# Attention with beacons, then a maxout FFN: three requests and two casts move one cluster up, and a batch's FFN units are dealt out in another order

## The chip, the cores and the metric

The kernel runs on one core of one Trainium2 chip. The metric is the device time of one execution in microseconds (us); lower is better. The kernel before takes 288.83 us, the median of three runs (288.78 to 288.86).

A core has TensorE (PE: matmuls, and the loads of their weights, PEld), VectorE (DVE), ScalarE (ACT) and GpSimd (POOL), each of which works through its own instructions in order, and SyncE (SP), which only asks for transfers. POOL asks for transfers too, for those that change the number type on the way. PSUM, where matmuls write, has eight banks of 512 fp32 columns; a bank can be written again when what stood in it has been read out by ACT or DVE.

## What is computed

```python
# attention: 8 batches, 8 heads, 576 tokens, 64 wide; 16 beacon keys and values ahead of the others
k_all = concat([beacon_k, k]);  v_all = concat([beacon_v, v])
scores = q @ k_all.T / sqrt(64), causal on the 576 keys
a = exp(scores - max);  a /= a.sum()
x = (a @ v_all) laid out as 4608 tokens x 512
# FFN: 512 -> 768 -> 512
h = maximum(maximum(x @ w1, x @ w2), x @ w3)
out = h @ w_out
```

## The kernel before

**Attention.** Two heads make a pair; there are 32 pairs, four to a batch, and two pairs make a quad. For a pair, q and k come in with tokens on partitions and have to be turned (head width on partitions) into the tiles `qT` and `kT`. `turn_pair` (L456) does it by 24 small matmuls with the identity into two PSUM banks; `evac_k` (DVE) and `evac_q` (DVE or ACT) copy them out. `place_beacons` (L445) puts 16 beacon columns ahead of `kT`. `emit_burst` (L522) computes all the scores of a pair in four groups, each in two neighbouring banks, and issues five exponentials on ACT. `emit_masks` (L540) zeroes on POOL what causality forbids. `emit_pv_whole` (L614) multiplies the weights of a quad with V into four banks, ACT copies the raw results and inverts the sums, and the returned `finish` multiplies the two on DVE into `xT`, the FFN's input.

Batch 0 goes by halves: `emit_pv` with `invert_sums` (ACT), which queues products, and `multiply` (DVE), which does them, out of banks 4 and 5. `finish_pv` is both in a row.

**FFN.** A unit is one PSUM result of the FFN: `mm1_unit` (L720), four matmuls of 512 tokens for one of six row blocks of `hT` and one of the three weights; `mm1_halves` (L731), the same work as two row blocks of 256 tokens, used for the first 512 tokens, half of which are there earlier; `mm2_unit` (L750), six matmuls with `w_out_sb`, whose result goes to the output. The first weight's result is cast into `hT`, the second's and third's are joined by `tensor_max` on DVE. With `end`, a unit is split over two banks that are evacuated one by one; in the main loop the last unit of each stretch is given that way, in the pair of banks that `last_pair` (L155) names. Each 512 tokens have 22 units; `units` (L794) lists them in the order in which they are given out, and `emit_ffn` gives out the next one. For the first 512 tokens: 0 to 5 are halves of the first 256 tokens, 6 to 11 of the others, 12 to 17 the third weight, 18 to 21 the second product, which needs `w_out_sb`.

**Order.** All of it is written out by hand: an engine does its instructions in the order in which the code issues them.

- `first_batch` (L903) does batch 0, with units between (`F`), turns pair 4, and asks for batch 1's V (`load_v`; the first of the two pieces stands behind a memset of DVE, its gate).
- `second_batch` (L988) runs a cluster for each of the pairs 4 to 7: beacons of the next pair, burst, masks, turning of the next pair, units (3, 3, 2, 2). Then follow the PV of quad 2, the turning of pair 8 and two units.
- The main loop (L1035) takes the pairs from 8 on: burst, a PV at every even pair, masks, then units; after the first unit the next pair is turned, after the second POOL casts and asks for later pairs. Pair 8 has two units, 18 and 19, with the turning of pair 9 between them.

**Transfers.** `load_cast(p)` (L252) asks on POOL for q and k of a pair, cast to bf16 on the way, into a place in `quad` tiles that the pair four before has left. Pairs 4 to 7 are asked for in `first_batch`. Pair 8 is asked for ahead of pair 7's masks, `w_out` (`load_w_out`, L344) and pair 9 behind the second of them. Batch 1's V lands in fp32 and POOL casts it into `v_sb` in two pieces (`cast_v`, L308): the first, row blocks 0 to 2, behind pair 6's masks, the second, blocks 3 and 4, behind pair 7's second mask. `next_load` then asks on SP for pairs 10 and 11, batch 2's V and pair 12; the first of these stands behind a memset of POOL, its gate.

Of the kernel before, what the change touches and what calls it, by code (L numbers as in the profile page):

```python
# [17 lines left out]
def kernel(  # L18
# [13 lines left out]
    nc = tc.nc  # L32
# [8 lines left out]
    n_ft = d_ff // 128  # L41
# [19 lines left out]
    PPB = H // 2  # L61
# [142 lines left out]
    by_act = nc.scalar.copy  # L204
# [482 lines left out]
    def finish_pv():  # L687
        invert_sums()
        multiply()
# [38 lines left out]
            else:  # L728
                (by_act if hi < TOKB else by_dve)(h[:, lo:hi], ps[:, lo:hi])  # L729

    def mm1_halves(tb, ft, i, lo, hi, new_ps):  # L731
        if tb not in hTs:
            hTs[tb] = ffn_h.tile([128, n_ft, TOKB], BF16, name="hT")
        h = hTs[tb][:, ft : ft + 2, lo:hi]
        ps = new_ps().rearrange("p (f c) -> p f c", f=2)
        for f in range(2):
            for ct in range(n_ct):
                nc.tensor.matmul(  # L738
                    ps[:, f],
                    w_in[i][:, ct, 128 * (ft + f) : 128 * (ft + f + 1)],  # L740
                    xT[:, ct, tb * TOKB + lo : tb * TOKB + hi],
                    start=(ct == 0),
                    stop=(ct == n_ct - 1),
                )
        if i == 0:
            by_dve(h, ps)
        else:
            nc.vector.tensor_max(h, h, ps)

    def mm2_unit(tb, tt, new_ps, end=False):  # L750
        hT = hTs[tb]
# [43 lines left out]
    for tb in range(n_tokb):  # L795
        need = 2 * ((TOKB * (tb + 1) - 1) // S) + 1
        if tb == 0:
            for n, lo in ((0, 0), (need, MID)):
                for i in range(2):
                    for ft in range(0, n_ft, 2):  # L800
                        units.append((n, mm1_halves, (tb, ft, i, lo, lo + MID)))
        for ft in range(n_ft):
            for i in range(2 if tb == 0 else 0, 3):
                units.append((need, mm1_unit, (tb, ft, i)))
        for tt in range(TOKB // 128):
            units.append((need, mm2_unit, (tb, tt)))
    END = len(units)
# [88 lines left out]

    S_, T, M, P, V = emit_scores, turn_part, emit_masks, emit_pv, cast_first_v

    def F(n=1, new_ps=ffn_psum.tile):
        for _ in range(n):  # L900
            assert emit_ffn(END, new_ps)

    def first_batch():  # L903
        S_(0, 0)
# [70 lines left out]
        M(3, 3, True)  # L975
        F()
        turn_beacons(1, B_PE, bk16_1)
        P(1, 1)
        finish_pv()
        F()  # L980
        turn_pair(PPB, by_act)
        load_v(1, 0, nc.vector)
        load_v(1, 1)
        place_beacons(PPB, by_act)
        F(2)
        free_banks[:] = [2, 3, 0, 1, 4, 5, 6, 7]

    def second_batch():  # L988
        for p in range(PPB, 2 * PPB):
            last = p == 2 * PPB - 1  # L990
            place_beacons(p + 1, by_act)
            emit_burst(p)
            if last:
                load_cast(2 * PPB)
            for gi in range(NG):
                emit_masks(p, gi)
                if last and gi == 1:
                    cast_v(1, 1, by_pool)
                    load_w_out()
                    load_cast(2 * PPB + 1)  # L1000
                    next_load(gate=nc.gpsimd)
                    next_load(4)
            if p == 2 * PPB - 2:
                cast_v(1, 0, by_pool)
            if not last:
                turn_pair(p + 1, by_dve)
            F(3 if p < PPB + 2 else 2, next_psum)
        finish = emit_pv_whole(n_quad)
        turn_pair(2 * PPB, by_dve)
        F(2, next_psum)  # L1010
        finish()
# [93 lines left out]
```

## Time and profile before

| | us |
|---|---|
| median of 3 runs | 288.83 |
| profiled execution, whole time | 290.4 |
| its span, first to last instruction | 288.7 |
| TensorE busy | 277.3 (96%) |
| DVE busy | 172.3 (60%) |
| ACT busy | 159.6 (55%) |
| POOL busy | 136.7 (47%) |

The mean granted TensorE clock is 0.994 of full speed. In the span, batch 0's end lies at about 25 to 31 us, the clusters of pairs 4 to 7 at 31 to 47, the PV of quad 2 at 47 to 50, pair 8 from 53 on and pair 9 from 64 on.

The profile is of one execution. A row of the timeline gives start, length, engine, line of the code, operation, output and inputs, sizes, and in brackets how long the engine had been idle and what ended that; neighbouring instructions of one line are merged in a row, with their count. A row of the waits gives who waited for whom, the total, how many times, and the longest. A row of the windows gives for a stretch the busy time and count of each engine, the granted clock, the mean busy share of the 16 DMA engines and the GB/s. A row of the DMA issues gives the size and the time from request to landing.

### The profile page before, as it was taken

To read this page: it belongs to the slowest core of one execution; us is meant where nothing else is said; L and a number is where in the kernel's file an instruction comes from. 1 tells how busy PE (TensorE), PEld (TensorE's weight loads), DVE (VectorE), ACT (ScalarE), POOL (GpSimd) and SP (SyncE) were. 2 spreads that over 40 slices of the span, in tenths; PEclk is the share of its full clock that TensorE was granted. 3 is DMA by queue.
4 is the path that set the end of the run, shared out by engine and by line. 5 is a ranking of instruction groups with operands and counts; after the bars stand their busy time and mean duration, and the time that the engine had idled before them with its cause. 6 is when DMAs were issued, how large, how long until landed. Compare 5 with 4: busy or idle time off the path is not lost.

```text
span 288.7 us, 7758 instructions
## 1 busy us (share of the span) xinstructions
PE 277.3 (96%) x3068; PEld 157.3 (54%) x3068; DVE 172.3 (60%) x303; ACT 159.6 (55%) x299; POOL 136.7 (47%) x282
## 2 busy tenths in 40 slices
PE   7889998879999999999999999999999999999995
PEld 3457764445555565555555787555555554444442
DVE  3774864537484748464836383638464847885873
ACT  3597586845859576666666666756675640000000
POOL 7298249628558592648465845584336210000000
PEclk9999999979999999999999999999999999999999
DMA  8999952999999799999999999899752003003004
GB/s 156 200 184 192 215 118 41 185 239 255 291 247 209 217 232 242 178 234 248 262 213 201 259 231 250 182 198 232 179 144 91 0 2 115 32 1 145 0 2 145
DMA packets 85316, 48.84 MB, mean 169 GB/s; under 512 B 64416, under 2 KB 80032, under 8 KB 85280
## 3 DMA queue, kind: packets, MB, share of 16 engines
q1 hardware_dynamic: 78176, 42.22, 64.5%
q0 software_dynamic: 6544, 5.80, 13.2%
q8 instruction: 24, 0.39, 0.6%
q10 hardware_dynamic: 560, 0.33, 0.5%
q14 instruction: 12, 0.10, 0.1%
HBM read 35.13 MB, written 14.22 MB: 171 GB/s over the span
## 4 chain that ended last, share of the span: by engine, by line
PE 85%; DMA 6%; POOL 2%; DVE 2%; issue 2%; ACT 1%; POOLq 0%; DVEq 0%; ACTq 0%
PE acc L709 44%; PE acc L757 16%; PE acc L633 9%; PE acc L513 7%; DMA quad<-in_k_dram 6%; PE acc L738 4%; PE acc L404 2%; PE acc L600 1%; DVE at_sb L551 1%; PE acc L498 1%; POOL quad L256 1%; POOL at_sb L553 1%; POOL v_sb L320 1%; ACT at_sb L531 0%; DVE kT L433 0%
## 5 line engine op out<-in xcount | busy, mean ns | idle before, releaser
L709 PE MATMUL acc<-xT,w_sb 128*128 128x512 bf16 (+4 forms) x744 | 135.5, 338 | 0.0
L553 POOL TENSOR_SCALAR_AFFINE_SELECT at_sb<-at_sb 128x256 bf16<-128x256 bf16 (+2 forms) x176 | 64.4, 386 | 85.8 <-ACT at_sb L531 79.6
L727 DVE TENSOR_TENSOR hT<-hT,acc 128x512 bf16<-128x512 bf16 x102 | 70.0, 687 | 58.4 <-PE acc L709 53.5
L709 PEld LDWEIGHTS <-w_sb 128*128 128x128 bf16 x744 | 69.1, 98 | 59.5
L531 ACT ACTIVATE at_sb<-acc 128x208 bf16<-128x208 f32 (+3 forms) x140 | 89.5, 737 | 8.2 <-PE acc L513 7.0
L757 PE MATMUL acc<-w_out_sb,hT 128*128 128x512 bf16 (+2 forms) x246 | 49.7, 355 | 0.8 <-DMA w_out_sb<-in_moe_w_out_dram 0.8
L764 DVE COPY y<-acc 128x512 f32<-128x512 f32 (+1 forms) x35 | 22.0, 629 | 23.9 <-PE acc L757 12.9
L275 POOL CAST p<-st 96x768 bf16<-96x768 f32 x44 | 35.0, 822 | 1.9 <-DMA st<-in_q_dram 1.0
L757 PEld LDWEIGHTS <-hT 128*128 128x128 bf16 x246 | 23.2, 100 | 23.2 <-DVE hT L727 1.6
L729 ACT CAST hT<-acc 128x352 bf16<-128x352 f32 x18 | 8.1, 452 | 47.3 <-PE acc L709 47.3
L729 DVE CAST hT<-acc 128x512 bf16<-128x512 f32 (+1 forms) x48 | 26.6, 554 | 9.7 <-PE acc L709 9.5
L513 PE MATMUL acc<-qT,kT 64*128 64x208 bf16 (+1 forms) x336 | 27.0, 282 | 0.9 <-DVE hT L727 0.4
L782 ACT COPY y<-acc 128x320 f32<-128x320 f32 x1 | 0.4, 426 | 46.0 <-PE acc L775 46.0
L633 PE MATMUL acc<-at_sb,v_sb 128*32 128x512 bf16 (+5 forms) x672 | 23.2, 281 | 0.6 <-POOL v_sb L320 0.6
L513 PEld LDWEIGHTS <-kT 64*128 64x128 bf16 x336 | 15.4, 94 | 13.6 <-issue 3.8
L656 DVE TENSOR_TENSOR xT<-raw,recip 128x576 bf16<-128x576 f32 x28 | 20.9, 788 | 0.0
L633 PEld LDWEIGHTS <-v_sb 128*32 128x32 bf16 (+1 forms) x672 | 14.5, 96 | 7.8 <-POOL v_sb L320 1.2
L320 POOL CAST v_sb<-st 128x1536 bf16<-128x1536 f32 (+2 forms) x21 | 18.2, 894 | 0.0
L643 ACT COPY raw<-acc 128x512 f32<-128x512 f32 x28 | 15.8, 637 | 3.7 <-PE acc L633 3.5
L507 ACT ACTIVATE at_sb<-acc 128x1024 bf16<-128x1024 f32 (+3 forms) x16 | 13.1, 859 | 3.9 <-PE acc L498 3.8
L633 PE MATMUL acc<-at_sb,ones 128*32 128x512 bf16 (+3 forms) x336 | 14.9, 284 | 0.0
L451 DVE COPY kT<-acc 128x576 bf16<-128x576 bf16 x12 | 9.0, 753 | 8.5 <-PE acc L404 8.5
(73 smaller groups left out, 178.7 us busy)
## 6 DMA issues: line engine op xcount, KB each, us to landing
out_dram<-y SPq DMA_DIRECT2D x35, 256.0 KB, 3.4
st<-in_q_dram SPq DMA_DIRECT2D x22, 288.0 KB, 4.5
st<-in_k_dram SPq DMA_DIRECT2D x22, 288.0 KB, 4.8
st<-in_v_dram SPq DMA_DIRECT2D x24, 256.0 KB, 6.4
w_sb<-in_moe_w_dram POOLq DMA_DIRECT2D x6, 384.0 KB, 6.7
q_dram<-p SPq DMA_DIRECT2D x16, 144.0 KB, 2.4
k_dram<-p SPq DMA_DIRECT2D x16, 144.0 KB, 2.2
st<-in_v_dram SPq DMA_DIRECT2D x8, 224.0 KB, 6.6
```

The lines of the kernel that those rows point to most:

```text
L275: cast(t16.rearrange("p r h d -> p h r d"), st[0:QP, i * NQ2 : (i + 1) * NQ2].rearrange("p (h r d) -> p h r d", h=2, r=QR),)
L320: cast(v_sb[0:n, t:t1].rearrange("p t h d -> p (t h d)"), st[0:n, (t - t_lo) * H * D : (t1 - t_lo) * H * D],)
L513: nc.tensor.matmul(ps, kTs[p % NT][hs, 128 * t : 128 * t + 128], qTs[p % NT][hs, q0:q1], start=True, stop=True, tile_position=(64 * e, 0),)
L531: nc.scalar.activation(out=both_heads(p, gi)[:, e0:e1], in_=acc[:, first + e0 : first + e1, 0 : g_width(p, gi)], func=AF.Exp, scale=scale,)
L553: nc.gpsimd.affine_select(out=view, in_=view, compare_op=ALU.is_ge, fill=0.0, base=x0, pattern=[[0, 2], [1, hi - lo]], channel_multiplier=-1,)
L633: nc.tensor.matmul(acc[32 * j : 32 * j + 32, bank, lo + q0 - qa : lo + qb - qa], lhsT, at_view(PPQ * quad + j // 2, t, j % 2, q0, qb), sta ...
L656: nc.vector.tensor_mul(xT[:, 2 * g + i, c0 : c0 + S], raw[:, i], recip)
L709: nc.tensor.matmul(ps[:, a:b], w_in[i][:, ct, 128 * ft : 128 * (ft + 1)], xT[:, ct, x0 : x0 + b - a], start=(ct == 0), stop=(ct == n_ct - 1),)
L727: nc.vector.tensor_max(h[:, lo:hi], h[:, lo:hi], ps[:, lo:hi])
L729: (by_act if hi < TOKB else by_dve)(h[:, lo:hi], ps[:, lo:hi])
L757: nc.tensor.matmul(ps[:, lo:hi], hT[:, ft, 128 * tt : 128 * (tt + 1)], w_out_sb[:, ft, lo:hi], start=(ft == 0), stop=(ft == n_ft - 1),)
L764: (by_act if hi < d_model else by_dve)(y[:, lo:hi], ps[:, lo:hi])
```

## The change

Pair 8 is asked for ahead of pair 5's masks, `w_out` and pair 9 ahead of pair 6's. V's first piece is cast behind pair 6's second mask, the second behind pair 6's last, and the gate with the loads behind it follows there. Of the first 512 tokens' units `first_batch` gives out five instead of six, and the clusters 3, 3, 3 and 2; in the first three clusters the last unit goes to two banks. For that `mm1_halves` gets the form `end`: one bank for each of its two row blocks, each evacuated by itself, the first weight's by ACT. The order of the units puts a half unit at each of these places. At the end of batch 0, beacons of pair 4 are placed ahead of the last PV, and the products of that PV are issued behind the turning of pair 4 and the loads of V, no longer ahead of a unit and the turning.

```diff
-    def mm1_halves(tb, ft, i, lo, hi, new_ps):
+    def mm1_halves(tb, ft, i, lo, hi, new_ps, end=False):
...
-        h = hTs[tb][:, ft : ft + 2, lo:hi]
-        ps = new_ps().rearrange("p (f c) -> p f c", f=2)
+        whole = None if end else new_ps().rearrange("p (f c) -> p f c", f=2)
         for f in range(2):
+            ps = new_ps()[:, 0 : hi - lo] if end else whole[:, f]
...
-        if i == 0:
-            by_dve(h, ps)
-        else:
-            nc.vector.tensor_max(h, h, ps)
+            if not end and f == 0:
+                continue
+            h = hTs[tb][:, ft + f, lo:hi] if end else hTs[tb][:, ft : ft + 2, lo:hi]
+            ps = ps if end else whole
+            if i > 0:
+                nc.vector.tensor_max(h, h, ps)
+            else:
+                (by_act if end else by_dve)(h, ps)
...
-            for n, lo in ((0, 0), (need, MID)):
-                for i in range(2):
-                    for ft in range(0, n_ft, 2):
-                        units.append((n, mm1_halves, (tb, ft, i, lo, lo + MID)))
-        for ft in range(n_ft):
-            for i in range(2 if tb == 0 else 0, 3):
-                units.append((need, mm1_unit, (tb, ft, i)))
+            order = [(0, f, 0) for f in (0, 2, 4)] + [(0, f, 1) for f in (0, 2, 4)]
+            order += [(MID, 0, 0), (MID, 2, 0), (MID, 0, 1), (MID, 2, 1), (MID, 4, 0)]
+            for lo, ft, i in order:
+                units.append((need if lo else 0, mm1_halves, (tb, ft, i, lo, lo + MID)))
+            for ft in range(n_ft):
+                units.append((need, mm1_unit, (tb, ft, 2)))
+            units.insert(len(order) + 2, (need, mm1_halves, (tb, 4, 1, MID, 2 * MID)))
+        else:
+            for ft in range(n_ft):
+                for i in range(3):
+                    units.append((need, mm1_unit, (tb, ft, i)))
...
-    def F(n=1, new_ps=ffn_psum.tile):
+    def F(n=1, new_ps=ffn_psum.tile, close=False):
         for _ in range(n):
-            assert emit_ffn(END, new_ps)
+            assert emit_ffn(END, new_ps, close)
...
         turn_beacons(1, B_PE, bk16_1)
+        place_beacons(PPB, by_act)
         P(1, 1)
-        finish_pv()
+        invert_sums()
         F()
         turn_pair(PPB, by_act)
         load_v(1, 0, nc.vector)
         load_v(1, 1)
-        place_beacons(PPB, by_act)
-        F(2)
+        multiply()
+        F()
...
         for p in range(PPB, 2 * PPB):
-            last = p == 2 * PPB - 1
             place_beacons(p + 1, by_act)
             emit_burst(p)
-            if last:
+            if p == PPB + 1:
                 load_cast(2 * PPB)
+            if p == PPB + 2:
+                load_w_out()
+                load_cast(2 * PPB + 1)
             for gi in range(NG):
                 emit_masks(p, gi)
-                if last and gi == 1:
-                    cast_v(1, 1, by_pool)
-                    load_w_out()
-                    load_cast(2 * PPB + 1)
-                    next_load(gate=nc.gpsimd)
-                    next_load(4)
-            if p == 2 * PPB - 2:
-                cast_v(1, 0, by_pool)
-            if not last:
+                if p == PPB + 2 and gi == 1:
+                    cast_v(1, 0, by_pool)
+            if p == PPB + 2:
+                cast_v(1, 1, by_pool)
+                next_load(gate=nc.gpsimd)
+                next_load(4)
+            if p + 1 < 2 * PPB:
                 turn_pair(p + 1, by_dve)
-            F(3 if p < PPB + 2 else 2, next_psum)
+                F(2, next_psum)
+                F(1, last_pair(), True)
+        F(2, next_psum)
         finish = emit_pv_whole(n_quad)
```

More of the change, by code (lines that the diff above doesn't have):

```diff
@@ L729, in mm1_unit @@
                 (by_act if hi < TOKB else by_dve)(h[:, lo:hi], ps[:, lo:hi])
-    def mm1_halves(tb, ft, i, lo, hi, new_ps):
+    def mm1_halves(tb, ft, i, lo, hi, new_ps, end=False):
         if tb not in hTs:
             hTs[tb] = ffn_h.tile([128, n_ft, TOKB], BF16, name="hT")
-        h = hTs[tb][:, ft : ft + 2, lo:hi]
-        ps = new_ps().rearrange("p (f c) -> p f c", f=2)
+        whole = None if end else new_ps().rearrange("p (f c) -> p f c", f=2)
         for f in range(2):
+            ps = new_ps()[:, 0 : hi - lo] if end else whole[:, f]
             for ct in range(n_ct):
                 nc.tensor.matmul(
-                    ps[:, f],
+                    ps,
                     w_in[i][:, ct, 128 * (ft + f) : 128 * (ft + f + 1)],
```

## The prediction

> **What bounds the kernel now.** I read the page first, then TensorE's waits, then the stretch in which they lie, in windows and instruction by instruction. "Cluster" is the work of one pair of heads in the loops of batches 1 and 2: burst of scores, five exponentials (ACT), masks (POOL), turning of the next pair, FFN units.
>
> ```profile
> span 288.7 us, 7758 instructions
> PE 277.3 (96%) x3068; PEld 157.3 (54%) x3068; DVE 172.3 (60%) x303; ACT 159.6 (55%) x299; POOL 136.7 (47%) x282
> ```
>
> TensorE is busy 96% of the span. Its waits between 40 and 72 us:
>
> ```profile
> PE acc L404 <- DMA quad<-in_k_dram: 1.2, 1, 1.2
> PE acc L757 <- DMA w_out_sb<-in_moe_w_out_dram: 0.8, 1, 0.8
> PE acc L633 <- POOL v_sb L320: 0.6, 2, 0.3
> ```
>
> The same view from 62 us to the end names no wait of TensorE at all. So what is won before 62 us is kept, as long as loads and casts come sooner by as much; what is won on another engine alone is worth nothing. The stretch in windows (PE, PEld, DVE, ACT, POOL busy, granted clock, DMA share, GB/s):
>
> ```profile
> 44.00:46.00 2.00, 1.80 (x16) 0.92 (x17) 0.88 (x2) 1.72 (x4) 2.00 (x4) 1.00 0.00 0
> ...
> 62.00:64.00 2.00, 2.00 (x14) 1.30 (x14) 0.11 (x2) 0.45 (x1) 0.00 (x0) 0.50 1.33 213
> ```
>
> The DMA engines stand still before the late requests are made, and after the waits the granted clock is 0.50. TensorE in order of time (start, length); L513 is a burst, L633 a PV, L404 a turning, L709 and L757 the FFN's two products:
>
> ```profile
> 43.92 0.81 PE L513 MATMUL acc<-qT,kT 64*128 64x208 bf16 x7
> ...
> 45.23 1.90 PE L709 MATMUL acc<-xT,w_sb 128*128 128x512 bf16 x8
> 47.07 0.86 PE L633 MATMUL acc<-at_sb,ones 128*32 128x512 bf16 x20
> ...
> 50.30 0.70 PE L404 MATMUL acc<-ident,quad 96*64 96x96 bf16 x24
> 50.94 1.90 PE L709 MATMUL acc<-xT,w_sb 128*128 128x512 bf16 x8
> 52.77 0.81 PE L513 MATMUL acc<-qT,kT 64*128 64x208 bf16 x7
> ...
> 54.08 0.87 PE L633 MATMUL acc<-at_sb,ones 128*32 128x512 bf16 x20
> ...
> 63.74 1.27 PE L513 MATMUL acc<-qT,kT 64*128 64x208 bf16 x12
> 64.94 1.47 PE L757 MATMUL acc<-w_out_sb,hT 128*128 128x512 bf16 x6
> 66.24 0.68 PE L404 MATMUL acc<-ident,p 96*128 96x96 bf16 x12
> ```
>
> And the same work where nothing disturbs it:
>
> ```profile
> 71.61 0.92 PE L513 MATMUL acc<-qT,kT 64*128 64x208 bf16 x12
> 72.46 0.86 PE L633 MATMUL acc<-at_sb,ones 128*32 128x512 bf16 x20
> ...
> 74.71 1.04 PE L709 MATMUL acc<-xT,w_sb 128*128 128x512 bf16 x4
> ```
>
> I count from start to start, since a matmul's tail hides the beginning of a wait: a burst takes 72.46 - 71.61 = 0.85, a PV 74.71 - 72.46 = 2.25, a unit of the second product 66.24 - 64.94 = 1.30, a turning from `quad` 50.94 - 50.30 = 0.64.
>
> **The requests made sooner.** Three terms.
>
> First, PV of quad 2 runs 50.30 - 47.07 = 3.23, 0.98 over 2.25: the two waits for batch 1's values. Now POOL casts them behind pair 7's first mask and ahead of its requests:
>
> ```profile
> 44.73 1.46 POOL L320 CAST v_sb<-st 128x1536 bf16<-128x1536 f32 x1
> ...
> 48.16 1.16 POOL L320 CAST v_sb<-st 128x512 bf16<-128x512 f32 x2
> 49.27 0.85 POOL L345 DMA_DIRECT2D w_out_sb<-in_moe_w_out_dram  x1
> ```
>
> After the change the first cast stands between pair 6's masks and the second right behind them. POOL then has, from the end of pair 5's masks, w_out's request (0.85), pair 9's two, two masks, 1.46, two masks, 1.16. Starting at about 40, with some 1.3 for pair 9's requests and 0.9 for two masks, the second cast ends at about 46.5, before TensorE is at the fourth row block of V (some 1.2 us into the PV). **-0.98**. Queued behind these on POOL are pair 7's masks and the memset that gates SP's loads of pairs 10 to 12 and batch 2's V: they come at about 47, now behind pair 9's requests and so after 51. Pair 6's masks are late by about 1 us, with no reader before 53. Pair 8's requests go ahead of pair 5's masks, in time that POOL spends waiting for exponentials; without that cover they would put the masks back by 1.3, which still nothing reads before 47.
>
> Second, from the start of quad 3's PV to pair 9's burst now takes 63.74 - 54.08 = 9.66: w_out is waited for, then pair 9's q and k, and the closing unit runs at half clock. Undisturbed it is 2.25 + 1.30 + 0.64 + 1.30 = 5.49. What the requests took to land:
>
> ```profile
> w_out_sb<-in_moe_w_out_dram POOLq DMA_DIRECT2D x1, 768.0 KB, 7.9
> ...
> quad<-in_k_dram POOLq DMA_DIRECT2D x1, 144.0 KB, 9.9
> ```
>
> Requested at 40 to 42 and landing at these times they are there by 52, and are needed at about 56 and 57. **-4.17**. Next in line is ACT, which must finish quad 2 and 3's sums before it can copy pair 9's qT:
>
> ```profile
> 58.11 0.68 ACT L651 ACTIVATE recip<-recip 128x576 f32<-128x576 f32 x1
> ...
> 63.04 0.45 ACT L764 COPY y<-acc 128x352 f32<-128x352 f32 x1 [2.74 <-PE acc L757]
> ```
>
> That chain began with pair 8's burst at 52.77 and ends 58.11 + 0.68 - 52.77 = 6.02 after it; a copy of 576 columns (0.75 on DVE, in a row below) brings it to 6.77, against 54.08 - 52.77 + 5.49 = 6.80 on TensorE. So TensorE just doesn't wait; the closing unit's 0.45 on ACT comes behind that copy and delays no one. If it did wait, I'd expect 0.2.
>
> Third, pair 9's burst at half clock took 64.94 - 63.74 = 1.20 for 0.85: **-0.35**, as the idle stretch ahead of it is gone.
>
> Pair 8's requests move into the time in which batch 1's V is being fetched:
>
> ```profile
> L304 SPq DMA_DIRECT2D st<-in_v_dram x5: 431/907/3907, 31.0 to 37.0; - x5
> ```
>
> ```profile
> st<-in_v_dram SPq DMA_DIRECT2D x1, 160.0 KB, 4.3
> ```
>
> ```profile
> quad<-in_k_dram POOLq DMA_DIRECT2D x1, 144.0 KB, 3.3
> ```
>
> The last piece of V, asked for at 37.0, lands at 41.3, and its cast is due at about 45.3; so I price this at nothing, with 4 us of cover. The two requests of pair 8 landed in 3.3 us each, over some 4 us together, with the engines to themselves. The Trainium skill ("DMA: Bandwidth & Descriptors", section "Issuing engines are not separate DMA queues") says that requests of different queues end up on the same 16 engines and interleave: by it V would land up to those 4 us later, at 45.3, and the sum would still be the same, with the cover used up; no run here yet shows the two together.
>
> **The end of batch 0 and the new order of units.** Units are only dealt out differently (five instead of six ahead of pair 4, then 3, 3, 3, 2), and a half unit of two products is as long as a whole unit, so TensorE's work is the same; what changes is who waits.
>
> ```profile
> 29.26 1.92 PE L738 MATMUL acc<-xT,w_sb 128*128 128x256 bf16 x16
> 31.11 1.21 PE L513 MATMUL acc<-qT,kT 64*128 64x208 bf16 x12
> ...
> 32.93 2.78 PE L738 MATMUL acc<-xT,w_sb 128*128 128x256 bf16 x24
> 35.65 0.68 PE L513 MATMUL acc<-qT,kT 64*128 64x208 bf16 x6
> ```
>
> ```profile
> 28.46 0.89 DVE L679 TENSOR_TENSOR xT<-acc,recip 128x288 bf16<-128x288 f32 x3 [1.63 <-ACT recip L669]
> ...
> 29.86 0.75 DVE L451 COPY kT<-acc 128x576 bf16<-128x576 bf16 x1
> ...
> 31.22 0.69 DVE L748 TENSOR_TENSOR hT<-hT,acc 128x512 bf16<-128x512 bf16 x1
> ```
>
> Today DVE does the products (0.89), a unit, kT, two units, done at 31.91, and the burst's last group starts behind that. After the change DVE begins with the unit, at about 28.8 (it ends on TensorE a turning, 0.64, before 29.26): 0.6 later comes kT, out at 30.15, so pair 4's burst starts at 30.2; then the three products, to about 30.96, and their banks hold the burst's third group; then the fifth unit's maximum, to 31.56, and its bank holds the fourth group, 0.3 long. The burst is over at about 31.9, and after the turning (0.64) units start at 32.55, against 32.93 now, with one unit of 0.9 fewer behind them. The reordering gives back most of what it seems to bring. The beacons' copy for pair 4 goes to where ACT waits for the PV; uncovered it would cost 0.15 (the row of two, below).
>
> In the clusters after that, exponentials set the pace:
>
> ```profile
> 29.65 0.31 ACT L447 COPY kT<-bT 128x16 bf16<-128x16 bf16 x2
> 31.47 3.19 ACT L531 ACTIVATE at_sb<-acc 128x208 bf16<-128x208 f32 x5 [1.51 <-PE acc L513]
> ```
>
> Units start 32.93 - 31.47 = 1.46 after the first exponential, which comes 0.36 after its burst, because they take the banks of its second group; then 35.65 - 32.93 = 2.72 to the next burst: 4.54 in all. The wait of the burst's last group for DVE lies inside that, and two banks at the end of a stretch don't shorten it. They put two 256-wide copies on ACT instead, ahead of the beacons and of the first exponential, in clusters 4 and 5. The trace has no such copy: it lies between a 16-wide (0.31 for two) and a 352-wide one (0.45). I take 0.37, the second one starting some 0.2 after the burst does (half of the 0.36 by which an exponential follows); starts overlap as in the row of two, so with the beacons between them the first exponential slips by 0.2. Bounds: 0 if all overlaps, 0.5 if nothing does. So bursts come at 32.55 + 2.72 = 35.27, + 4.74 = 40.01, + 4.74 = 44.75, against 43.92 now with as many units done: 0.83 later. Pair 7's burst, with two 256-wide maxima ahead of it (0.41 each, between 0 and the 0.69 of a whole one), takes about 1.02 instead of 45.23 - 43.92 = 1.31. **+0.54**, with bounds of -0.3 (no bank held, no slip) and +1.6.
>
> **Sum.** -0.98 - 4.17 - 0.35 + 0.54 = -4.96. It is a difference inside one profiled execution, which took 290.4 with a span of 288.7; the runs' median, 288.83, is 0.1 above that span, so I take it off the median: 288.83 - 4.96 = **283.9**.
>
> **Rivals.**
> *The second batch costs more than I gave it*: all slips at their upper bounds, +1.1, so 285.0. For it: ACT has only some 0.7 us free in a cluster there (4.54 less 3.19 and about 0.6 of copies). Against it: ACT's instructions overlap in every row above.
>
> *The half clock stays in another place.* TensorE would wait briefly, and more often, in clusters 4 to 6, as above. One spell at 0.50 cost about 1.7 here (0.35 in the burst, and some 1.3 in the closing unit before it, which takes 1.30 at full clock): 285.6. Against it: between 44 and 46 TensorE also paused, at a granted clock of 1.00. The Trainium skill ("TensorE: Matmul & The Clock Gate", section "A second HAM failure mode: psum-queue depth-cycling") tells of just that, short pauses between groups that make the clock swing to half; the trace so far doesn't bear it out.
>
> *Slower than before: V becomes late.* Suppose the DMA engines serve POOL's requests ahead of SP's. Then what is left of V when pair 8 is asked for waits for pair 8, w_out and pair 9, until about 52; the second cast would end at 53.2, 4.8 after the 48.4 at which TensorE wants it, and with the half clock after such idling (1.7) the time is 283.9 + 6.5 = 290.4. It is slower from some 3.8 us of idling on, with V landing after 51. Against it:
>
> ```profile
> st<-in_q_dram SPq DMA_DIRECT2D x1, 288.0 KB, 6.7
> ```
>
> This load of SP's, asked for right behind pair 9's k, landed in 6.7 us where that took 9.9.
>
> **How the numbers follow.** Forecast 0.76 (own range 283.2 to 284.8), costlier second batch 0.13, half clock 0.06, V late 0.05. The bounds of the slips and the second rival put the top at 285.6; at the bottom the slips at their lower bound give 283.0, and a little for waits that I count too short. What differs by 0.2% (0.6 us) can be told from no change: faster 0.94, within 0.2% 0.01, slower 0.05.
>
> **What would show it.** No wait of TensorE for w_out, `quad` or v_sb between 40 and 62; granted clock 1.00 there; quad 2's PV 2.25 long and starting a little later than 47.07; pair 9's burst near 59.2; pair 4's burst starting near 30.2 but over one microsecond long; ACT's 256-wide copies ahead of the exponentials of pairs 5 and 6. Wrong would make it: a cast of v_sb with a DMA wait before it; pair 9's burst waiting for qT on ACT by more than 0.2; a wait of TensorE after 62 that was not there.

## The result: faster, by half of what was forecast

| | before | after |
|---|---|---|
| median, us | 288.85 (6 runs, 288.41 to 289.7) | 286.2 (6 runs, 285.62 to 287.6) |
| profiled execution, its span | 290.4, 288.7 | 286.34, 284.6 |
| ratio after / before | | 0.9914 [0.9886, 0.9942] |

The time fell by 2.65 us, not by 4.96, and 286.2 lies above the range that was given and above the 285.6 that was put as its top. The kernel before, timed twice on one chip (first experiment), came out 0.35% apart: the 0.2% that the prediction took for what can be told from no change was too fine.

In every run of this study the time is the span plus 1.7 us. The span that belongs to the median of before is therefore 287.1, and the profiled execution's 288.7 was 1.6 longer than that.

**Where the steps landed.** TensorE after the change, in order of time (start, length, line, operation, idle time before it):

```profile
26.41 0.27 PE L360 MATMUL acc<-ident,bk 48*128 48x48 bf16 x4
...
30.98 1.12 PE L513 MATMUL acc<-qT,kT 64*128 64x208 bf16 x6
32.32 0.38 PE L513 MATMUL acc<-qT,kT 64*128 64x336 bf16 x6 [0.22 <-DVE hT L750]
33.27 2.79 PE L738 MATMUL acc<-xT,w_sb 128*128 128x256 bf16 x24
35.99 0.89 PE L513 MATMUL acc<-qT,kT 64*128 64x208 bf16 x12
...
40.65 0.89 PE L513 MATMUL acc<-qT,kT 64*128 64x208 bf16 x12
...
45.47 1.00 PE L513 MATMUL acc<-qT,kT 64*128 64x208 bf16 x12
...
48.23 0.86 PE L633 MATMUL acc<-at_sb,ones 128*32 128x512 bf16 x20
...
50.49 0.70 PE L404 MATMUL acc<-ident,quad 96*64 96x96 bf16 x24
...
54.26 0.86 PE L633 MATMUL acc<-at_sb,ones 128*32 128x512 bf16 x20
...
56.51 1.47 PE L761 MATMUL acc<-w_out_sb,hT 128*128 128x512 bf16 x6
57.91 0.70 PE L404 MATMUL acc<-ident,quad 96*64 96x96 bf16 x24
58.54 1.49 PE L761 MATMUL acc<-w_out_sb,hT 128*128 128x352 bf16 x12
59.96 0.91 PE L513 MATMUL acc<-qT,kT 64*128 64x208 bf16 x12
60.81 1.47 PE L761 MATMUL acc<-w_out_sb,hT 128*128 128x512 bf16 x6
```

and the row of the profile before with which the first one is to be compared:

```profile
25.66 0.27 PE L360 MATMUL acc<-ident,bk 48*128 48x48 bf16 x4
```

L360 is the turning of batch 1's beacons, the last thing ahead of the change. It stands 0.75 later here, for a reason that lies ahead of all that the change touches (below), so I count each step from it:

| from the beacons' turning, or within the step | before | forecast | after |
|---|---|---|---|
| burst of pair 4 | 5.45 | 4.54 | 4.57 |
| units of the next cluster | 7.27 | 6.89 | 6.86 |
| burst of pair 5 | 9.99 | 9.61 | 9.58 |
| burst of pair 6 | 14.58 | 14.35 | 14.24 |
| burst of pair 7 | 18.26 | 19.09 | 19.06 |
| PV of quad 2, start | 21.41 | 21.95 | 21.82 |
| PV of quad 2, length | 3.23 | 2.25 | 2.26 |
| PV of quad 3 to burst of pair 9 | 9.66 | 5.49 | 5.70 |
| burst of pair 9 | 1.20 | 0.85 | 0.85 |
| closing unit behind that burst | 39.28 | 34.32 | 34.40 |

The last row is the whole change: 4.88 us are gone between the beacons and pair 9's closing unit, of 4.96 in the sum. From that unit to the end the two executions take 223.73 and 223.82: nothing is given back later. TensorE's waits between 26 and 70 us name neither w_out nor `quad` nor v_sb any more:

```profile
PE acc L709 <- ACT at_sb L531: 0.4, 1, 0.4
PE acc L738 <- ACT at_sb L531: 0.4, 1, 0.4
PE acc L513 <- DVE hT L750: 0.2, 1, 0.2
PE acc L513 <- DVE hT L727: 0.2, 1, 0.2
PE acc L404 <- ACT at_sb L531: 0.2, 1, 0.2
```

So the working held, and the time did not. What the sum was taken off is the difference. The page's line of granted clock, in 40 slices, of the profile before (7.2 us to a slice):

```profile
PEclk9999999979999999999999999999999999999999
```

and after:

```profile
PEclk9979999999999999999999999999999999999999
```

Each profiled execution has one stretch at half clock, but in different places: the ninth slice before, the third after. Windows around it (PE, PEld, DVE, ACT, POOL busy, granted clock, DMA share, GB/s), before:

```profile
57.74:61.15 3.41, 1.84 (x30) 0.90 (x29) 0.69 (x1) 1.76 (x5) 1.64 (x2) 1.00 1.15 274
...
61.15:64.55 3.40, 3.40 (x19) 1.91 (x20) 1.40 (x3) 0.81 (x3) 0.00 (x0) 0.50 1.31 216
64.60:65.10 0.50, 0.50 (x9) 0.30 (x6) 0.50 (x2) 0.50 (x2) 0.27 (x1) 1.00 0.91 164
```

and after:

```profile
12.79:16.20 3.41, 2.07 (x32) 1.05 (x32) 3.16 (x12) 2.27 (x4) 1.51 (x3) 1.00 1.27 236
...
16.20:19.60 3.40, 3.35 (x62) 1.84 (x64) 1.47 (x5) 2.35 (x4) 3.31 (x9) 0.51 1.03 176
```

A spell is 3.41 us long, and 3.41 x 0.5 / 288.7 = 0.006, so it leaves a mean granted clock of 0.994, which is what both executions have. That number is given for every run and tells roughly which executions had a spell. It is not exact: half clock in the last microseconds, when TensorE has nothing left to do, lowers the mean too and costs nothing. In the profile of "before again" (first experiment) it is 0.50 from 287.4 us to the end at 288.9, with no matmul in that time; that alone is 0.003, so a mean of 0.997 need not be a spell that cost anything.

### The profile page after: what moved, and what is told of

Read it like the earlier page. It is cut to its first block, busy times and chain, and to the rows that moved or that the text cites. A ratio compares the mean times of both kernels' runs of the same rounds, so it can differ in the third digit from the quotient of the medians.

```text
span 284.6 us, 7756 instructions
## 1 busy us (share of the span) xinstructions
PE 276.3 (97%) x3068; PEld 157.2 (55%) x3068; DVE 171.6 (60%) x302; ACT 161.2 (57%) x303; POOL 136.3 (48%) x282
## 3 DMA queue, kind: packets, MB, share of 16 engines
q0 software_dynamic: 6544, 5.80, 13.2%
## 4 chain that ended last, share of the span: by engine, by line
PE 91%; DVE 4%; DMA 2%; ACT 1%; issue 1%; DVEq 0%
PE acc L709 46%; PE acc L761 16%; PE acc L633 11%; PE acc L513 8%; PE acc L738 4%; PE acc L600 2%; PE acc L404 2%; DMA bk<-in_beacon_k_dram 2%; DVE at_sb L551 1%; PE acc L498 1%; ACT at_sb L531 1%; DVE kT L433 1%; DVE qT L433 1%; PE acc L779 0%; PE acc L425 0%
## 5 line engine op out<-in xcount | busy, mean ns | idle before, releaser
L761 PE MATMUL acc<-w_out_sb,hT 128*128 128x512 bf16 (+2 forms) x246 | 48.5, 348 | 0.0
L761 PEld LDWEIGHTS <-hT 128*128 128x128 bf16 x246 | 22.5, 98 | 21.9 <-DVE hT L727 1.8
L513 PE MATMUL acc<-qT,kT 64*128 64x208 bf16 (+1 forms) x336 | 26.3, 279 | 0.5 <-DVE hT L750 0.2
```

What stands on the lines that cost most here:

```text
L513: nc.tensor.matmul(ps, kTs[p % NT][hs, 128 * t : 128 * t + 128], qTs[p % NT][hs, q0:q1], start=True, stop=True, tile_position=(64 * e, 0),)
L761: nc.tensor.matmul(ps[:, lo:hi], hT[:, ft, 128 * tt : 128 * (tt + 1)], w_out_sb[:, ft, lo:hi], start=(ft == 0), stop=(ft == n_ft - 1),)
```

## The experiments

**The two kernels again, and each half of the change alone.** The first two are the kernels before and after, unchanged, timed in more rounds.

> The kernel before, unchanged, to see other executions of it. The profile the prediction was made from took 290.4 us (span 288.7, 1.7 around it), 1.55 over the median of 288.85, and had one spell of 3.4 us at a granted clock of 0.50 right behind its wait for pair 9. Theory A, the prediction's sum was taken off the wrong time: other executions have the same waits but not the spell in that place; then the median is again about 288.9, spans lie near 287.1 with a mean clock of 1.000 or a spell elsewhere, and from the start of quad 3's PV to pair 9's burst it is 9.66 less 1.4, about 8.3, with 0.85 for the burst. Theory B, the waits themselves are shorter in most executions: that stretch is under 7.5. Theory C, all executions of the kernel before are like the profiled one, and the changed kernel loses 2 us somewhere: 9.66 and 1.20 again.

> The changed kernel, unchanged, to see other executions of it. Its profile has no wait of TensorE for w_out, for the quads or for v_sb, and its steps from the end of batch 0 on came out within 0.15 us of the prediction's; a spell of half clock lay in batch 0 (16.2 to 19.7 us) and cost about 0.75 there. Theory A: median about 286.2, all steps from batch 0's end on again as in that profile, and the spread of its runs (285.6 to 287.6) comes from ahead of that end. Theory C: a second profile shows waits or longer steps behind 31 us that the first did not show, 1 to 2 us in all.

The third has the requests and casts where the change puts them, with the old units, order and copies:

```diff
+            if p == PPB + 1:
                 load_cast(2 * PPB)
+            if p == PPB + 2:
+                load_w_out()
+                load_cast(2 * PPB + 1)
...
+                if p == PPB + 2 and gi == 1:
+                    cast_v(1, 0, by_pool)
+            if p == PPB + 2:
+                cast_v(1, 1, by_pool)
+                next_load(gate=nc.gpsimd)
+                next_load(4)
```

> The requests and the casts of V moved up, everything else as before (order of units, one bank for a closing unit, end of batch 0). The prediction's sum gives the move -0.98 for quad 2's PV and about -2.8 for w_out and pair 9 without the half clock (-4.5 with it), and the rest of the change +0.41 as its profile measured at the start of quad 2's PV. Theory A: quad 2's PV starts 21.4 us after batch 1's beacons are turned, as in the kernel before (47.07 - 25.66), against 21.8 in the changed one; PV 2.25 long; no wait for w_out or quad; time 0.4 under the changed kernel, about 285.8. If the rest of the change is needed for the gain (the cast of V or POOL's masks late without it), PV of quad 2 takes over 2.5 or starts later than 21.8.

The fourth is the other half: the changed units, order and copies, with the requests and casts back where they were.

> The order of units, two banks for closing units and the new end of batch 0, with requests and casts where they were. By the prediction's step for this part (+0.54 forecast, +0.41 measured) quad 2's PV starts about 0.4 later after the beacons' turning than before (21.8 for 21.4), the casts of V and the requests follow ACT's exponentials and are late by the same, so the waits for V, w_out and pair 9 stay and the time is 289.0 to 289.4. If the two banks and the order bring something by themselves, the time is under 288.6.

| kernel | median, us | ratio to before | PV of quad 2 | PV of quad 3 to burst of pair 9 | burst of pair 9, from the beacons |
|---|---|---|---|---|---|
| before again | 290.69 (12 runs) | 1.0035 [1.0004, 1.0066] | 3.23 | 9.45 | 37.86 |
| after again | 285.83 (6) | 0.9891 [0.9852, 0.9931] | 2.25 | 5.70 | 33.56 |
| requests alone | 285.93 (6) | 0.9872 [0.9843, 0.9902] | 2.25 | 5.70 | 33.27 |
| units alone | 290.64 (12) | 1.0024 [0.9991, 1.0057] | 2.79 | 8.47 | 36.87 |

The requests carry the gain; the rest brings nothing that can be measured, and in this pair of profiles it costs 0.3 (33.56 against 33.27); a second profile of the requests alone, below, has 33.94 for another reason. "Units alone" still waits for both transfers, as TensorE's waits between 38 and 75 us of that kernel say:

```profile
PE acc L404 <- DMA quad<-in_k_dram: 1.3, 1, 1.3
PE acc L761 <- DMA w_out_sb<-in_moe_w_out_dram: 0.9, 1, 0.9
```

but it has no spell behind them, and so 8.47 where before has 9.66. "Before again" was no execution without a spell, as I had expected it to be: it had one at 62.1, near the old place, and its median came out 1.9 above the one I had started from. So what an execution without a spell looks like has to come from the clocks of the runs and from the kernels below. The runs of the kernel before, all those taken beside the experiments and the 12 of "before again", sorted by their mean granted clock:

| mean clock | runs | median, us | lowest to highest |
|---|---|---|---|
| 0.998 and more | 34 | 288.88 | 287.89 to 290.55 |
| 0.994 to 0.997 | 32 | 289.86 | 288.93 to 291.16 |
| 0.990 to 0.993 | 8 | 290.7 | 290.36 to 290.88 |
| 0.989 and less | 12 | 291.07 | 290.54 to 292.28 |

Four runs in ten of the kernel before have next to no half clock. The clocks of the three runs from which the prediction took its 288.83 are not on record, but all three (288.78 to 288.86) lie under 288.93, the lowest of the 52 runs with a mean clock under 0.998; the profiled 290.4 lies among the runs that have some. By the same count the changed kernel, in its 12 runs, has 8 at 0.998 and more, with a median of 285.83: 3.05 below 288.88. Three runs near 288.8 were a lucky draw, too: the median of all 86 is 289.52, and that of the changed kernel's 12 is 286.05, 3.5 lower. Over these runs, which come from several chips, the gain is thus nearer 3.5 than the 2.65 of the first six, and still well under 4.96.

**Filling TensorE's waits.** The kernel before, with matmuls of a constant operand in the two waits for w_out and pair 9 (they go to banks that are free and are read by nobody), so that TensorE doesn't idle there:

```diff
-    def turn_pair(p, q_copy):
+    def turn_pair(p, q_copy, idle=(0, 0)):
...
+            fill(at[i], idle[i])
...
+            if p == 2 * PPB:
+                fill(free_banks[0], 3)
...
-                    turn_pair(p + 1, by_act)
+                    turn_pair(p + 1, by_act, (2, 5) if p == 2 * PPB else (0, 0))
```

> The kernel before, with ten 512-wide matmuls of constants put where TensorE waits for w_out (3), pair 9's q (2) and k (5), into banks that the next instruction takes anyway; they change no result and should fit into the waits. Theory A says that the half-clock spell behind this wait comes from TensorE standing idle, costs about 1.65 us and is in some executions only (runs of the kernel before so far: about 288.7 at a mean granted clock of 1.000, about 290.0 at 0.994, 291 at 0.986). Then: profile without a spell between 55 and 70, from quad 3's PV to pair 9's burst 8.2 to 8.5, burst 0.85, waits for w_out and quad still bounding it (fills end, then TensorE waits on), and runs of about 288.7 with a narrower spread. If the spell has another cause, it is still there and runs are as before or later.

The waits stay, and this profile has no spell at the old place; "units alone" had none there either, without a fill, so one profile doesn't show that the fill took it away. It does show the waits without half clock. Windows of that kernel at the old place:

```profile
60.00:62.00 2.00, 1.97 (x21) 0.96 (x20) 0.33 (x1) 0.69 (x2) 1.02 (x2) 1.00 1.14 258
62.00:64.00 2.00, 2.00 (x24) 1.28 (x23) 1.35 (x4) 1.19 (x4) 0.09 (x1) 1.00 1.32 197
```

The granted clock is 1.00 throughout, and from quad 3's PV to pair 9's burst it takes 8.20. The waits alone are thus worth 8.20 - 5.70 = 2.50 here; of the 4.17 in the sum, some 1.46 was the half clock. The times don't show it: 289.53, ratio 1.0012 [0.998, 1.0044], because 5 of its 12 runs still have spells (mean clocks of 0.986 to 0.994, 289.4 to 292.4); where, only the profiled one could show.

**Taking away the spells in batch 0.** There are two waits of TensorE between 12 and 16 us, the stretch ahead of the spell in the changed kernel. Six constant matmuls in them, in the changed kernel and in the one with requests alone:

```diff
+        fill(6, 4)
         S_(0, 1)
...
+        fill(7, 2)
         S_(0, 3)
```

> The changed kernel, with six 512-wide matmuls of constants in batch 0, four ahead of the scores for which TensorE waits 0.8 to 0.9 for kT (at 13.7 us) and two ahead of those for which it waits 0.6 for ACT (at 15.0). Theory A says that spells of half clock in batch 0 (15.4 to 22 in its two profiles) follow those waits and make up the rest of the spread: then the profile has no spell there, batch 1's beacons are turned at about 25.7 instead of 26.4 and 27.9, and all runs lie near 285.5. If the spells have another cause, they stay, and the beacons' time is as before or up to 0.3 later.

> Requests and casts moved alone, as in the third run, with the same six matmuls of constants in batch 0. Theory A: no spell in batch 0, beacons at about 25.7, pair 9's burst 33.3 after them, span 283.5, all runs near 285.2, the fastest of all versions. Else as the third run, 285.9.

The changed kernel so filled has the beacons at 25.78, in a second profile (below) at 25.52, and the burst of pair 9 33.57 behind it as ever. Its windows where the spell was:

```profile
16.00:18.00 2.00, 1.89 (x66) 1.28 (x58) 1.68 (x4) 1.56 (x3) 1.99 (x5) 1.00 1.21 202
18.00:20.00 2.00, 1.70 (x62) 1.07 (x50) 0.80 (x3) 1.97 (x5) 1.99 (x6) 1.00 0.93 179
```

In the 12 runs of these two kernels the mean clock never fell under 0.999. Their medians are 286.38, ratio 0.9892 [0.9851, 0.9932], and 285.86, ratio 0.9857 [0.9813, 0.9901], no better than without the fills: the 0.75 us that the spell costs can be seen in the trace and not in the times. One reason is that other runs are long without a spell (288.18, and one of 289.82 at a clock of 0.999). Another stands in the profile of the requests alone, filled. Its beacons are at 25.70, but pair 9's burst comes 33.94 behind them, not the 33.3 expected, because batch 0's last PV waits for a mask:

```profile
27.07 0.48 PE L600 MATMUL acc<-at_sb,ones 128*32 128x208 bf16 x6 [0.44 <-POOL at_sb L553]
```

POOL, which comes to these masks at 26.60 here and at 26.37 without the fills, is no sooner for TensorE's gain: pair 4's burst starts at 31.96, against 32.04 without the fills.

The same fills on both sides, so that neither has a spell in batch 0, and the wait filled as well in the kernel before:

> The kernel before with both sets of constant matmuls (ten in the wait for w_out and pair 9, six in batch 0), so that no window of TensorE is idle enough for a spell of half clock. Theory A: mean clock 0.999 to 1.000 in all runs and a median of 288.6 to 288.9; against the next kernel, which is the changed one without spells, the difference is the gain of the change with the clock left out, 3.2 (from the profiles: 0.99 in quad 2's PV, 8.20 to 8.40 less 5.70 behind it, less 0.43), 2.9 to 3.5. If the gain is really near the 5.0 forecast, this median is above 290; if other waits vary, the difference is under 2.7.

> The changed kernel with the six constant matmuls in batch 0, again, on the same chip as the run before. Mean clock 0.999 to 1.000 in all runs, median 285.4 to 286.4 as in the first such run (286.38), 2.9 to 3.5 under the run before.

289.32 (12 runs) against 285.74 (6), a gain of 3.58 between kernels that have no spell in 17 of 18 runs. That is a little more than the 2.9 to 3.5 forecast for it; the kernel before was longer than expected, and its profiled execution waited longer for pair 9's k (asked for at 51.2, landed at 62.5), so that quad 3's PV to pair 9's burst took 9.76 with no half clock in it. How long that transfer takes differs between executions of one kernel; why wasn't tried.

**The casts alone.** The kernel before with both casts of batch 1's V moved a cluster ahead, the requests left:

```diff
+                if p == PPB + 2 and gi == 1:
+                    cast_v(1, 0, by_pool)
+            if p == PPB + 2:
+                cast_v(1, 1, by_pool)
```

> Only batch 1's casts of V moved (to pair 6's masks), requests where they were. By the prediction's terms quad 2's PV is 2.25 instead of 3.23; the request for w_out comes 1.16 sooner, as POOL has no cast ahead of it, TensorE comes 0.98 sooner, so the waits for w_out and pair 9 stay within 0.3 and pair 9's burst is about 1.0 to 1.2 sooner after the beacons' turning than the kernel before would have it without a spell (36.6), at 35.4 to 35.6; with a spell behind the wait 1.3 more. If the waits for V only hid other waits, it is at 36.4 or more.

The first term by itself: quad 2's PV takes 2.28, and only the waits for the transfers remain; one of the two for pairs' k is new, 0.24 for pair 8. From TensorE's waits of that kernel:

```profile
PE acc L757 <- DMA w_out_sb<-in_moe_w_out_dram: 0.6, 1, 0.6
PE acc L404 <- DMA quad<-in_k_dram: 1.7, 2, 1.4
```

w_out and pair 9 are asked for sooner here too, since they stand behind the casts on POOL, but not soon enough: 8.40, and pair 9's burst at 36.29, later than the 35.4 to 35.6 I had expected. Against the 36.6 that I had put for the kernel before without a spell, only 0.3 of the 0.98 is left: TensorE then waits for the transfers instead.

**Why the second batch costs 0.4.** First the closing half units' copies back on DVE, then the old order of the products:

```diff
-                (by_act if end else by_dve)(h, ps)
+                by_dve(h, ps)
```

> The changed kernel with the closing halves of the first weight (clusters of pairs 4 and 5) cast by DVE instead of ACT. The prediction put 0.2 per cluster on ACT's two copies ahead of the exponentials. If so, clusters 5 and 6 take 4.55 to 4.6 instead of 4.65 and 4.83 from burst to burst, and quad 2's PV starts 21.5 to 21.6 after the beacons' turning instead of 21.83. If ACT's copies cost nothing, or DVE's casts hold the burst's last group by as much, it stays within 0.1 of 21.83.

```diff
         invert_sums()
+        multiply()
         F()
         turn_pair(PPB, by_act)
...
-        multiply()
```

> The changed kernel with the products of the last PV of batch 0 again ahead of the unit and the turning (five units kept). The prediction said that the burst of pair 4 starts sooner with the products behind, but waits inside for their banks, so that the order brings little. Measured in the changed kernel: burst at 4.58 after the beacons' turning, next burst at 9.59. By that step the old order has the burst start at 5.0 to 5.1, with shorter waits inside, and the next burst at 9.3 to 9.5. If the new order helps, the next burst comes at 9.7 or later.

Without ACT's copies the bursts of pairs 5 to 7 are 4.54 and 4.51 apart instead of 4.66 and 4.82, and quad 2's PV starts 21.41 behind the beacons, exactly as before, instead of 21.82. That is the whole of what the second batch costs. The order of the products moves pair 4's burst (5.03 instead of 4.57) and not the next one (9.56 instead of 9.58).

The kernel with copies on DVE showed something else as well. Its quad 2's PV takes 4.08 (POOL in order of time, from 40 us):

```profile
40.23 0.85 POOL L345 DMA_DIRECT2D w_out_sb<-in_moe_w_out_dram  x1
...
43.05 1.47 POOL L320 CAST v_sb<-st 128x1536 bf16<-128x1536 f32 x1
45.56 0.60 POOL L320 CAST v_sb<-st 128x512 bf16<-128x512 f32 x1
50.04 0.61 POOL L320 CAST v_sb<-st 80x512 bf16<-80x512 f32 x1 [3.87 <-DMA st<-in_v_dram]
```

and the reason stands in the requests of V on SP and in their landing (first and last start; then the median from issue to landing) of the same kernel:

```profile
L304 SPq DMA_DIRECT2D st<-in_v_dram x5: 736/1472/4770, 31.0 to 39.0; - x5
```

```profile
st<-in_v_dram SPq DMA_DIRECT2D x1, 160.0 KB, 11.0
```

In the profile before SP asked for V's last piece at 37.0 and it landed after 4.3 us. Here it asks at 39.0, 1.3 us ahead of w_out's request, and the piece takes 11.0. In the changed kernel as profiled that load takes 5.6, and the second cast doesn't wait. In the seven profiles with w_out asked for in that place and SP 2.4 to 3.4 us ahead of it, the changed kernel's among them, the piece lands after 5.6 to 6.5. The execution in which it took 11.0 was 287.61 long, at a clock of 1.00. The changed kernel has such times at full clock too (287.27 and 287.6 of the first six, 287.95 and 288.18 among the filled ones), so I tried the mechanism both ways.

**w_out and pair 9 behind V, and ahead of it.** One kernel asks for w_out behind V's first cast and for pair 9 behind the second (it also has the copies on DVE, the old order of products and the fills in batch 0); the other asks for both a cluster sooner still:

```diff
-            if p == PPB + 2:
-                load_w_out()
-                load_cast(2 * PPB + 1)
...
                     cast_v(1, 0, by_pool)
+                    load_w_out()
             if p == PPB + 2:
                 cast_v(1, 1, by_pool)
+                load_cast(2 * PPB + 1)
```

> The changed kernel with w_out asked for behind V's first cast and pair 9 behind its second (the cluster is the same, but both stand behind the casts on POOL), closing halves cast by DVE, the products of batch 0's last PV ahead again, and the six constant matmuls in batch 0. Theory D: in about one execution in six of the changed kernel V's last piece is asked for late by SP (at 39 instead of 37) and then lands behind w_out and pair 9, 11 us later, POOL waits for it and quad 2's PV is 1.8 longer, as in the profile with closing casts on DVE (PV 4.08). Then here, with no request of POOL's ahead of V's casts but pair 8's, no run lies over 287; quad 2's PV at 21.4 after the beacons, pair 9's burst at 33.1, median 285.2 to 285.6. If V's lateness has nothing to do with these requests, runs of 287 to 288 at a clock of 1.000 stay (about one in six), or w_out or pair 9 is waited for.

```diff
             if p == PPB + 1:
                 load_cast(2 * PPB)
-            if p == PPB + 2:
                 load_w_out()
                 load_cast(2 * PPB + 1)
```

> The changed kernel with w_out and pair 9 asked for a further cluster sooner, right behind pair 8, ahead of pair 5's masks (at 37 to 39 us). Theory D: they now meet V in every execution; V's pieces land 4 to 8 us later than 42.8, POOL waits for them in its casts, quad 2's PV takes over 3 us, and the median is 287.5 to 290. If V's lateness in that one profile had another cause, PV is 2.25 as in the changed kernel and the median 285.8 to 286.4.

POOL in the first of them:

```profile
43.50 0.85 POOL L345 DMA_DIRECT2D w_out_sb<-in_moe_w_out_dram  x1
45.46 1.16 POOL L320 CAST v_sb<-st 128x512 bf16<-128x512 f32 x2
46.57 0.64 POOL L256 DMA_DIRECT2D quad<-in_q_dram  x1
```

and in the second:

```profile
35.91 0.87 POOL L345 DMA_DIRECT2D w_out_sb<-in_moe_w_out_dram  x1
...
47.95 1.31 POOL L320 CAST v_sb<-st 128x512 bf16<-128x512 f32 x2 [3.09 <-DMA st<-in_v_dram]
```

The first took 286.05, ratio 0.9866 [0.9834, 0.9897]: no faster in the median than the change (285.2 to 285.6 was expected), but with the shortest span of all profiles (283.46) and no run over 286.12, where the changed kernel, filled or not, has 6 of 24 at 287 or more (2 of these at clocks of 0.985 and 0.986). Six runs are few: with 4 in 22 long at full clock, none in six would come about 30 times in 100. Its w_out is asked for 3.5 us later than in the change, counted from the beacons, and still nothing waits for it. The second took 288.12, ratio 0.9935 [0.9903, 0.9967]. In its one profile V's last piece now takes 11.4 us with SP asking in time (at 37.2), the cast waits 3.09, and quad 2's PV takes 2.87. That is a loss of 0.6. The 288.12 has half clock in it as well: 5 of its 12 runs have mean clocks under 0.998, and the other seven have a median of 286.34, 0.5 above the changed kernel's 285.83. So a load of SP's is held up by POOL's requests in flight beside it: 11.0 and 11.4 us in the two profiles where w_out is asked for 1.3 us behind it or 1.2 ahead of it, against 5.6 to 6.5 above.

## Why the prediction was half right

**The first two terms held where they were worked out.** "-0.98" for quad 2's PV measured 0.97 to 0.99; "-4.17" for quad 3's PV to pair 9's burst measured 3.96, because I counted 5.49 for what takes 5.70 when nothing waits: the unit of the second product and the closing unit take 1.40 and 1.42 from start to start (56.51 to 57.91, 58.54 to 59.96), where I counted 1.30 for each. Why they take a tenth more was not tried. "So TensorE just doesn't wait" for ACT's sums, with 0.03 to spare, is right: none of the waits above is pair 9's.

**The second batch was right in size and cause.** "+0.54" measured 0.41 to 0.43. "The reordering gives back most of what it seems to bring" is shown by the old order of products, and the slip of "0.2" for each stretch closed with two copies on ACT by taking these away (0.12 and 0.31).

**The step that failed is the sum's last one**: "the runs' median, 288.83, is 0.1 above that span, so I take it off the median". That compares a time with a span: a run's time is its span and 1.7, so the time that goes with 288.7 is 290.4. The execution I had taken apart was 1.55 slower than the median, and the excess lay in the very stretch I was costing: its spell of half clock, counted as gain at 0.35 (the third term) and inside the 4.17 (some 1.3 of it, as the second rival says itself; 1.2 to 1.5 by three of the four profiles without a spell there, which have 8.20 to 8.47; the fourth is longer for its transfer). The three runs behind that median are as fast as those with next to no half clock, so there was little half clock in them for a change to take away. Without it the sum is -0.98 - 2.6 + 0.43 = -3.2 (2.6 from 8.20 to 8.47 less 5.70), against 3.05 between the medians at full clock and 3.58 with the fills. Or taken the other way, off the execution that it was made from, it gives 290.4 - 4.96 = 285.4; the changed kernel's profiled 286.34, less the 0.75 by which its beacons are late, is 285.6.

**Whether V makes up the rest of the shortfall is open.** The difference between 3.2 and 2.65 is within the interval of the ratio, 1.7 to 3.3 us. Of the first six runs two were at 287.3 and 287.6 at full clock. In the repeat none was, and the median was 285.83 instead of 286.2. That these two waited for V is not shown, as they have no profile; it is shown that such an execution of a near relative did, and that the one profile with w_out and pair 9 asked for sooner still did; and the six runs with w_out and pair 9 behind the casts have no long one among them.

**Of the rivals**, "V becomes late" did not happen in any of the changed kernel's four profiles, two of them filled; two relatives show a lateness like it, at another price. It needs no strict order of POOL's requests ahead of SP's: a piece asked for 2 us late, or with 1 MB of requests ahead of it, lands after 11 us, and costs 1.8 or 0.6 in quad 2's PV, where the rival's price was 4.8. "4 us of cover" was worked out from one execution's SP, which asked at 37.0; others ask at up to 39.5. The Trainium skill ("DMA: Bandwidth & Descriptors", section "Issuing engines are not separate DMA queues") has the requests of all engines interleave on the same 16 DMA engines; the 11.4 us of the last experiment against 4.3 agree, and with less in flight the rule cost nothing. "The half clock stays in another place" was right in the profiled execution, but the place, 16.2 us, lies ahead of all that the change touches; in clusters 4 to 6 no profile of the changed kernel has a granted clock under 1.00, whatever TensorE's short waits there.

**Open**: why SP asks for V's last piece 10.8 us behind the beacons in one profile and 13.2 in another (36.8 to 39.5 us into the span); the long landing of pair 9's k in the filled kernel before; the run of 289.82.

## What to carry to other kernels

Before a sum made in a profiled execution is taken off a median, compare that execution's own time with it: if it is longer, look for the excess first (here the line of granted clock and a mean of 0.994), and don't count as gain what the median never paid. A load moved ahead competes with everything that is then in flight; ask for it behind what is needed sooner, as late as nobody waits for it, which here cost nothing. A copy moved to an engine that sets the pace of a loop, ACT in these clusters, cost its slip each time round, 0.1 and 0.3 us.

## What was not expected of the hardware

The half clock comes in spells of one length, 3.41 us (one of 6.8 in the repeat of the changed kernel), not for as long as TensorE waits: in the windows shown above TensorE was busy 1.84 and 2.07 us of the 3.41 before, and no wait in the first of them was longer than 1.2. The trace's clock records change on a grid of that length: full clock from 5.99 and half clock from 16.23 to 19.65 us in the changed kernel, three windows and one; from 6.53 and from 61.14 to 64.56 before, sixteen and one. The Trainium skill ("TensorE: Matmul & The Clock Gate", section "What's actually happening") has a free-running window of 3413 ns, which the length bears out; its table asks for an idle window for the half clock, and here a window half idle was enough. TensorE's busy time alone gives no limit: a window with 2.41 us of it was followed by half clock (requests alone, 11.55 to 14.96), and one with 1.92 was not (units alone, 59.11 to 62.52).

Whether there is a spell differs from execution to execution of the same kernel, as the four groups of clocks above show. That fits a window that doesn't start with the kernel: full clock began between 4.5 and 7.5 us into the span. Six constant matmuls in two waits kept the clock at 0.999 and more in all 18 runs of the changed kernel and of the requests alone that had them; the kernel before, filled, had one run of 12 at 0.994.
